# Fused attention, expert and gated layers: when the kept halves come back, where the second batch's k and the probabilities are made, and one place for a tile's transposes

## The chip, the cores and the metric

One core of a Trainium2 chip runs the whole program. The metric is the device time of one execution in microseconds, lower is better. Runs of this kernel lie within 0.5 us of each other.

## The reference

Three layers follow one another. The inputs are float32, and 2304 tokens (4 batches of 576) pass through all three.

```python
# attention: q, k, v are (4, 8, 576, 64); k and v are averaged over groups of 8 positions (576 -> 72)
k_p = k.reshape(B, H, 72, 8, D).mean(axis=3);  v_p = v.reshape(B, H, 72, 8, D).mean(axis=3)
scores = q @ k_p.T / sqrt(64);  attn = softmax(scores);  x = attn @ v_p      # -> (2304, 512)
# four experts, each token weighted by its probabilities
p = domain_probs / (domain_probs.sum(-1, keepdims=True) + 1e-9)              # (2304, 4)
for e in range(4):
    out += p[:, e:e+1] * (relu(x @ w1[e]) @ w2[e])                           # 512 -> 1024 -> 512
# gated layer
h = ((x @ w1) * (x @ w2)) @ w3;  result = h @ w_out                          # 512 -> 1024 -> 512
```

## The kernel before, in words

Every product is formed from a high and a low part of each operand (`mm3`, lines 111 to 114: three matmuls for one), so that a matrix has two tiles, `...h` and `...l`. The high part is a copy on ScalarE (ACT), the low part a subtraction on VectorE (DVE) or GpSimd (POOL): `hi_lo`, lines 116 to 118, whose line 118 thus shows up for many tiles.

**Lead and hooks.** Tokens go in blocks of 384, three tiles of 128. `lead` is a list of pieces that makes the first block's attention before any expert work: pooled k (`pool_k`: DVE sums groups of 8, POOL multiplies with a mask into `kb`), its transposes (`make_kT`, TensorE), transposed q (`make_qT`), scores, exponentials, normalisation, the transposes of the probabilities (`attn_T`, reached by `do_turn`), and `attend`, which gives the block's operand `xh`, `xl`. Tile 3 is the first of the next block, and tile 4 the first that needs the second batch's pooled k (`k1`, `kT1`). Its q needs a load that interleaves rows (`load_qb`) and one transpose on DVE (line 388).

The expert work goes in units: (expert, block, one of 8 column chunks `fc`). A unit makes 12 matmuls of the first product (`expert_h`, lines 568 to 573, result `hhh`, `hhl`) and, two units later, 12 of the second. Between these halves of units lie the numbered `hooks`: `between(n)` runs what was put into hook n, so that the remaining attention work fills in among the expert matmuls. All work on one engine runs in the order in which the program is written. Loads are issued from SyncE's queue (SP) in the order of the list `loads`, which follows the order of lead and hooks. In the hooks and in all the gated layer's set-up only two PSUM banks (`spare[:2]`) are left for scores, kT and transposes of probabilities.

**The w stage** (units of kind "w", around 887 to 935 us) multiplies w3 with w_out while the operands of the gated layer's first product are prepared: `weights_of(j, 0)` and `weights_of(j, 1)` split four blocks of weights into parts; the second of these calls splits a tile `s` of 128 x 1024 into `wh`, `wl`, four times in this stage. In every unit DVE also makes `w3hl`, which the unit's second matmul (line 113) reads.

**The gated layer** takes the 4 batches twice, for two halves of the inner dimension. In the first half a batch's tiles (4 or 5 of 128 x 512) are written to `half_d` in memory; in the second half each is loaded again (`earlier`), added on DVE to the tile's PSUM result and stored to `out` (`give`). The tiles' matmuls are run for three of four chunks for all tiles, then tile by tile for the fourth, each followed by its `give`. `rawpool` has four buffers.

The functions that the change touches:

Of the kernel before, what the change touches and what calls it, by code (L numbers as in the profile page):

```python
# [17 lines left out]
def fused_kernel(  # L18
# [246 lines left out]
    with tc.manual_schedule():  # L265
# [57 lines left out]
            nc.sync.dma_start(r[:NK, :], v[b, h].rearrange("(j r) d -> j (r d)", r=POOL))  # L323
            in_t["v", b, h] = r

        def pool_k(b, c):
            if c == 0:
                kb_t[b] = ap.tile([P, NCH, 2, D], F32, tag="kb", name="kb", bufs=1)
            r, n = in_t.pop(("k", b, c))
            kp = ap.tile([P, D], F32, tag="kp", name="kp")  # L330
            if n < P:
                nc.gpsimd.memset(kb_t[b][n:, c], 0.0)
            nc.vector.tensor_reduce(kp[:n], r[:n, :].rearrange("p (r d) -> p d r", d=D), axis=AX.X, op=ALU.add)  # L333
            nc.gpsimd.tensor_tensor(kb_t[b][:n, c], kp[:n].unsqueeze(1).broadcast_to([n, 2, D]),
                                    mk[:n, c].unsqueeze(2).broadcast_to([n, 2, D]), op=ALU.mult)

        def make_kT(b, g0, g1):
            if g0 == 0:
                kT_t[b] = ap.tile([P, NCH * P], F32, tag="kT", name="kT")
            pt = bank("kT_ps")  # L340
            for c in range(g0, g1):
                nc.tensor.transpose(pt[:, (c - g0) * P:(c - g0 + 1) * P],
                                    kb_t[b][:, c].rearrange("p a d -> p (a d)"), ident)
            nc.scalar.activation(kT_t[b][:, g0 * P:g1 * P], pt[:, :(g1 - g0) * P], AF.Copy)
# [117 lines left out]
            if what:  # L462
                done(what)

        def do_k(b):
            return [(("k", b, c), lambda c=c: pool_k(b, c)) for c in range(NCH)]

        def do_kT(b):
            return [(None, lambda: make_kT(b, 0, 4)), (None, lambda: make_kT(b, 4, NCH))]

        def do_v(b, *engs):
            return [(("v", b, h), lambda h=h: pool_v(b, h, engs[h % len(engs)])) for h in range(H)]
# [33 lines left out]
        def weight(eng):  # L506
            return [(None, lambda: stream.split(eng))]
# [4 lines left out]
        def warm(n):  # L512

            def f():
                pw = bank("warm")
                for _ in range(n):
                    nc.tensor.transpose(pw[:, :P], ident, ident)
            return [(None, f)]

        k0, kT0, k1, kT1 = do_k(0), do_kT(0), do_k(1), do_kT(1)  # L520
        v0 = do_v(0, GP, GP, VE, GP, GP, GP, GP, GP)
        lead = (warm(W0) + k0[:4] + kT0[:1] + k0[4:] + do_qT(0) + kT0[1:] + do_qT(1) + do_scores(0) + do_exps(0) + v0[:2]
                + do_qT(2) + do_scores(1) + v0[2:3] + do_exps(1) + do_scores(2) + v0[3:5] + do_normalise(0) + do_exps(2)
                + v0[5:6] + do_normalise(1) + warm(W1) + do_turn(0) + do_normalise(2, VE) + v0[6:]
                + warm(W2) + do_turn(1) + weight(GP) + do_turn(2) + do_attend(0) + weight(VE) + k1[:2] + do_qT(3))

        hooks = [[] for _ in range(2 * FC * ATT_BLOCKS + 4)]
        hooks[1] = k1[2:] + do_qT(TPB + 1)
        hooks[2] = kT1[:1]
        hooks[3] = kT1[1:] + [(None, probs)]  # L530
        hooks[5] = [(None, probs_T)]
        for t in range(TPB, NTILE + 1):
            h = hooks[3 * (t - TPB) + (t > TPB):]
            if t < NTILE:
                h[0] += do_scores(t) + do_exps(t)
                if t > TPB:
                    h[1] += do_qT(t + 1)
                one, two = do_normalise(t)
                h[1].append(one)
                h[2].append(two)  # L540
            if t > TPB:
                one, two = do_turn(t - 1)
                h[1].insert(0, one)
                h[2].insert(0, two)
                if t % TPB == 0:
                    h[3] += do_attend(t // TPB - 1)
        for b, at_v, at_k in ((1, 3, None), (2, 15, 11), (3, 26, 23)):
            for n, piece in enumerate(do_v(b, GP)):
                hooks[at_v + n].append(piece)
            if at_k:  # L550
                for n, piece in enumerate(do_k(b)):
                    hooks[at_k + n // 2].append(piece)
                hooks[at_k + 4] += do_kT(b)
        first = [("k", 0, c) for c in range(NCH)] + [("q", t) for t in range(LEAD)] + [("v", 0, h) for h in range(H)]
        loads += first + [what for what, _ in lead + sum(hooks, []) if what and what not in first]

# [82 lines left out]
        def weights_of(j, n=None):  # L639

            def split(src, at, m, eng):
                src = src.rearrange("p a b c -> p (a b c)") if len(src.shape) == 4 else src.rearrange("p a c -> p (a c)")
                hi_lo(*(t[:, at:at + m].rearrange("p a b c -> p (a b c)") for t in wop_t[j]), src, eng)

            if n != 1:
                left, right = gate_t.pop(j) if j in gate_t else (r for r, _ in stream.take(2))
                wop_t[j] = tuple(late["wops"].tile([P, 7, 2, P], F32R, tag=t, name=t) for t in ("wh", "wl"))
                s = parts[j] = late["small"].tile([P, 4, 2, P], F32, tag="t", name="s", bufs=2)
                sub, add = ALU.subtract, ALU.add
                nc.vector.tensor_tensor(s[:, 0], right[:, :2], right[:, 2:], op=add)  # L650
                nc.vector.tensor_tensor(s[:, 1], s[:, 0], left[:, :2], op=sub)
                nc.vector.tensor_tensor(s[:, 2], left[:, :2], right[:, :2], op=sub)
                nc.vector.tensor_tensor(s[:, 3], left[:, 2:], s[:, 1], op=sub)
                split(left, A11, 2, nc.vector)
                split(right[:, 2:], A22, 1, nc.vector)
                stream.fill()
            if n != 0:
                split(parts.pop(j), S1, 4, nc.gpsimd)

        xr_t, xo_t, xo_next, sums_t, stores = {}, {}, {}, {}, []  # L660
        B0, T0 = slice(B11, B22 + 1), slice(T1, T4 + 1)
# [140 lines left out]
        def made(u):  # L802

            kind, key, fc = u
            if kind == "e":
                e, i = key
                if e == 0 and i == 0:
                    if fc + LAG < FC:
                        stream.split(nc.vector)
                    stream.split()  # L810
                if i == NB - 1:
                    stream.split()
                if e == 0 and i == ATT_BLOCKS and fc == 3:
                    enter_late()
                if dec and fc in (4, 5, 6, 7):
                    rounding.step(SCRATCH + 4 * FC)
                if e == E - 1:
                    if i == NB - 1 and fc == 0:
                        rounding.flush()
                        assert rounding.finished()  # L820
                        stream.fill()
                    if i > 0 and fc == 4:
                        store_acc(i - 1)
                    if i == NB - 1 and fc == FC - 1:
                        enter_wide()
# [127 lines left out]
        for half in range(2):  # L953
            for b in range(B):
# [34 lines left out]
                if b % 2:  # L989
                    tiles = tiles[1:] + tiles[:1]  # L990
                banks = [bank_r("g2") for _ in tiles]
                halves = {}

                def run(m, js):
                    t, get = tiles[m]
                    for j in js:
                        wh, wl = w34_t[half * NJ + j]
                        g = get(j)
                        mm3(banks[m], g[:, 0], g[:, 1], wh[:, 0], wl[:, 0], j == 0, j == NJ - 1)

                def give(m):
                    t, _ = tiles[m]
# [12 lines left out]
                        nc.sync.dma_start(half_d[t], ob)  # L1015

                def earlier(m):
                    if half and m < len(tiles):
                        halves[m] = rawpool.tile([P, DM], F32, tag="raw", name="half")
                        nc.sync.dma_start(halves[m], half_d[tiles[m][0]])  # L1020

                earlier(0)
                earlier(1)
                if half == 0 and b < B - 2:
                    for kc in range(2):
                        load_x(acc_d, b + 2, kc)
                for m in range(len(tiles)):
                    run(m, range(NJ - 1))
                for m in range(len(tiles)):
                    run(m, [NJ - 1])  # L1030
                    give(m)
                    if swap and m in (1, 3):
                        weights_of(2 + m // 2)
                    earlier(m + 2)
                    if m == 1:
                        put_away()
                if not last:
# [37 lines left out]
```

## Time and profile before

| what | value |
|---|---|
| median of 3 runs | 1226.5 us (1226.33 to 1226.85) |
| the profiled execution | 1226.71 us, of which its span is 1225.0 us |
| TensorE matmul busy (PE) | 1198.9 us, 98% of the span |
| TensorE weight load busy (PEld) | 1152.3 us, 94% |
| DVE / POOL / ACT busy | 667.6 / 369.3 / 277.6 us |
| mean granted clock of TensorE | 0.996 of full speed |

TensorE is the busy engine. What another engine does costs time only where TensorE waits for it, where the first matmuls have to wait for their operands, or behind the last matmul. So the places to read are the few in which PE is not busy, and what it waits for there.

### The profile page before, as it was taken

To read this page: it belongs to the slowest core of one execution; us is meant where nothing else is said; L and a number is where in the kernel's file an instruction comes from. 1 tells how busy PE (TensorE), PEld (TensorE's weight loads), DVE (VectorE), ACT (ScalarE), POOL (GpSimd) and SP (SyncE) were. 2 spreads that over 40 slices of the span, in tenths; PEclk is the share of its full clock that TensorE was granted. 3 is DMA by queue.
4 is the path that set the end of the run, shared out by engine and by line. 5 is a ranking of instruction groups with operands and counts; after the bars stand their busy time and mean duration, and the time that the engine had idled before them with its cause. 6 is when DMAs were issued, how large, how long until landed. Compare 5 with 4: busy or idle time off the path is not lost.

```text
span 1225.0 us, 18777 instructions
## 1 busy us (share of the span) xinstructions
PE 1198.9 (98%) x7089; PEld 1152.3 (94%) x7089; DVE 667.6 (54%) x1489; ACT 277.6 (23%) x535; POOL 369.3 (30%) x432
## 2 busy tenths in 40 slices
PE   7899999999999999999999999999998999999996
PEld 6799989999999999999999999999987999999995
DVE  6887544444444556454444444444287767775453
ACT  4443331131111113111112211111253333231110
POOL 5764300043222236222225522211422222341121
PEclk9999999999999999999999999999999999999999
DMA  8853102143112245222114322123365443944642
GB/s 202 230 143 95 52 5 69 56 131 101 52 42 59 59 101 153 59 57 49 49 52 128 108 84 81 56 84 102 110 217 177 155 169 122 338 166 170 217 155 68
DMA packets 147758, 138.47 MB, mean 113 GB/s; under 512 B 48524, under 2 KB 114644, under 8 KB 147668
## 3 DMA queue, kind: packets, MB, share of 16 engines
q1 hardware_dynamic: 147668, 137.28, 36.8%
q8 instruction: 55, 0.90, 0.3%
q14 instruction: 35, 0.29, 0.1%
HBM read 96.05 MB, written 41.19 MB: 112 GB/s over the span
## 4 chain that ended last, share of the span: by engine, by line
PE 90%; DVE 4%; DMA 2%; POOL 1%; issue 1%; ACT 1%; SPq 1%; DVEq 0%; POOLq 0%; ACTq 0%
PE g L113 24%; PE g L114 24%; PE g L112 24%; PE s L112 5%; PE s L114 5%; PE s L113 5%; PE x_ps L447 1%; PE at_ps L435 1%; PE sc L401 1%; DVE w3hl L118 1%; DMA raw<-w 1%; DMA half<-half 0%; POOL w2l L118 0%; DMA stacc<-in_v_dram 0%; DVE kp L333 0%
## 5 line engine op out<-in xcount | busy, mean ns | idle before, releaser
L572 DVE SCALAR_TENSOR_TENSOR hhl<-g,hhh 128x384 fp32r<-128x384 f32 x192 | 106.7, 556 | 365.1 <-ACT hhh L571 365.0
L112 PE MATMUL g<-xl,w1h 128*128 128x384 f32 x768 | 261.5, 340 | 0.5 <-DVE xl L118 0.5
L113 PE MATMUL g<-xh,w1l 128*128 128x384 f32 x768 | 260.0, 339 | 0.0
L112 PE MATMUL g<-hhl,w2h 128*128 128x384 f32 x768 | 259.7, 338 | 0.2 <-DVE part L592 0.2
L114 PE MATMUL g<-xh,w1h 128*128 128x384 f32 x768 | 259.7, 338 | 0.0
L113 PE MATMUL g<-hhh,w2l 128*128 128x384 f32 x768 | 258.0, 336 | 0.0
L114 PE MATMUL g<-hhh,w2h 128*128 128x384 f32 x768 | 257.9, 336 | 0.0
L571 ACT ACTIVATE hhh<-g 128x384 fp32r<-128x384 f32 x192 | 94.5, 492 | 579.6 <-PE g L114 553.7
L224 POOL TENSOR_TENSOR dtmp<-dtmp 128x256 f32<-128x256 f32 x80 | 58.8, 735 | 407.5 <-DVE dtmp L223 366.3
L112 PEld LDWEIGHTS g<-xl,w1h 128*128 128x128 f32 x768 | 144.6, 188 | 2.0 <-DVE xl L118 1.8
L112 PEld LDWEIGHTS g<-hhl,w2h 128*128 128x128 f32 x768 | 144.2, 188 | 0.9 <-DVE part L592 0.7
L113 PEld LDWEIGHTS g<-xh,w1l 128*128 128x128 f32 x768 | 144.7, 188 | 0.0
L114 PEld LDWEIGHTS g<-xh,w1h 128*128 128x128 f32 x768 | 144.5, 188 | 0.0
L113 PEld LDWEIGHTS g<-hhh,w2l 128*128 128x128 f32 x768 | 144.4, 188 | 0.0
L114 PEld LDWEIGHTS g<-hhh,w2h 128*128 128x128 f32 x768 | 144.1, 188 | 0.0
L118 POOL TENSOR_TENSOR g<-c,g 128x576 fp32r<-128x576 f32 x32 | 47.4, 1481 | 193.9 <-ACT g L117 193.9
L593 POOL TENSOR_TENSOR acc<-acc,part 128x384 f32<-128x384 f32 x72 | 71.2, 1021 | 72.0 <-DVE part L592 72.0
L112 PE MATMUL s<-xol,wh 128*128 128x288 f32 x308 | 91.1, 296 | 0.0
L114 PE MATMUL s<-xoh,wh 128*128 128x288 f32 x308 | 91.0, 296 | 0.0
L113 PE MATMUL s<-xoh,wl 128*128 128x288 f32 x308 | 90.6, 294 | 0.0
L117 ACT ACTIVATE g<-c 128x576 fp32r<-128x576 f32 x32 | 21.9, 686 | 160.5 <-DVE c L947 160.5
L112 PEld LDWEIGHTS s<-xol,wh 128*128 128x128 f32 x308 | 57.9, 188 | 0.4
(146 smaller groups left out, 1790.7 us busy)
## 6 DMA issues: line engine op xcount, KB each, us to landing
raw<-in_moe_w_dram SPq DMA_DIRECT2D x64, 256.0 KB
din<-in_moe_w_dram SPq DMA_DIRECT2D x64, 256.0 KB
p<-p SPq DMA_DIRECT2D x24, 192.0 KB
acc<-acc SPq DMA_DIRECT2D x6, 768.0 KB
xr<-acc SPq DMA_DIRECT2D x16, 288.0 KB
half<-ob SPq DMA_DIRECT2D x18, 256.0 KB
half<-half SPq DMA_DIRECT2D x18, 256.0 KB
out_dram<-half SPq DMA_DIRECT2D x18, 256.0 KB
```

Source lines behind the costliest of these rows:

```text
L112: nc.tensor.matmul(ps, lh, rl, start=first, stop=False)
L113: nc.tensor.matmul(ps, ll, rh, start=False, stop=False)
L114: nc.tensor.matmul(ps, lh, rh, start=False, stop=last)
L117: nc.scalar.activation(hi, src, AF.Copy)
L118: (lo_eng or nc.vector).tensor_tensor(lo, src, hi.bitcast(F32), op=ALU.subtract)
L224: nc.gpsimd.tensor_tensor(a, a, b, op=ALU.add)
L401: nc.tensor.matmul(sc[off:off + n, (hp % 2) * W:(hp % 2 + 1) * W], qT[:, hp, off:off + n], kT_t[b][:, hp * W:(hp + 1) * W], start=True, st ...
L435: nc.tensor.transpose(pt[:NK, g * P:(g + 1) * P], e[:, half * G + g, :], ident)
L447: nc.tensor.matmul(px[a * D:(a + 1) * D, off:off + n], vp_t[b][:NK, 2 * hp + a], at_t[i, hp // 2][:NK, 2 * (hp % 2) + a, off:off + n], sta ...
L571: nc.scalar.activation(hh, ps, AF.Relu)
L572: nc.vector.scalar_tensor_tensor(hl, ps, 0.0, hh.bitcast(F32), op0=ALU.max, op1=ALU.subtract)
L593: nc.gpsimd.tensor_tensor(acc_t[i][:, c], acc_t[i][:, c], part, op=ALU.add)
```

## The change

Six things change. (1) In the lead, the four DVE operations on the probabilities and their transpose (`probs`, `probs_T`) and tile 3's q transpose go ahead of block 0's `attend`; the first three chunks of `k1` go there too and are summed on POOL, by three additions each, in place of one DVE reduction. (2) kT1 is made in pieces of 3 and 2 chunks at hooks 3 and 4 (before: 4 and 1 at hooks 2 and 3), and tile 4's q transpose moves from hook 1 to 3. (3) In the hooks a table `at` sets the place of each tile; the two halves of a tile's transposes stand in one hook, two after the next tile's scores, and the transposes of kT for batches 2 and 3 have hooks without transposes of probabilities. `enter_late` comes one unit later, as attention ends five hooks later. (4) In the w stage the low part of the 128 x 1024 split goes from POOL to DVE. (5) In the second half of the gated layer all of a batch's kept halves are loaded at the batch's begin, four into `rawpool` and the fifth into a buffer of `small`. (6) The last tile of all is made in two pieces of 256 columns, each with its own PSUM bank, addition and store.

```diff
-        def pool_k(b, c):
+        def pool_k(b, c, eng=nc.vector):
...
-            nc.vector.tensor_reduce(kp[:n], r[:n, :].rearrange("p (r d) -> p d r", d=D), axis=AX.X, op=ALU.add)
+            if eng is nc.vector:
+                eng.tensor_reduce(kp[:n], r[:n, :].rearrange("p (r d) -> p d r", d=D), axis=AX.X, op=ALU.add)
+            else:
+                eng.tensor_tensor(r[:n, :256], r[:n, :256], r[:n, 256:], op=ALU.add)
+                eng.tensor_tensor(r[:n, :128], r[:n, :128], r[:n, 128:256], op=ALU.add)
+                eng.tensor_tensor(kp[:n], r[:n, :64], r[:n, 64:128], op=ALU.add)
...
-        k0, kT0, k1, kT1 = do_k(0), do_kT(0), do_k(1), do_kT(1)
+        k0, kT0, k1, kT1 = do_k(0), do_kT(0), do_k(1, 3), do_kT(1, 3)
...
-                + warm(W2) + do_turn(1) + weight(GP) + do_turn(2) + do_attend(0) + weight(VE) + k1[:2] + do_qT(3))
+                + warm(W2) + do_turn(1) + weight(GP) + do_turn(2) + [(None, probs), (None, probs_T)] + do_qT(3) + k1[:3] + do_attend(0)
+                + weight(VE))
...
-        hooks[1] = k1[2:] + do_qT(TPB + 1)
-        hooks[2] = kT1[:1]
-        hooks[3] = kT1[1:] + [(None, probs)]
-        hooks[5] = [(None, probs_T)]
...
+        hooks[1] = k1[3:]
+        hooks[3] = kT1[:1] + do_qT(TPB + 1)
+        hooks[4] = kT1[1:]
+        at = {TPB: 0, TPB + 1: 5, TPB + 2: 8}
+        for i in range(2, NB):
+            for n, gap in enumerate((-3, 0, 3)):
+                at[i * TPB + n] = 10 * i - 6 + gap
...
+        for t in range(TPB, NTILE):
+            hooks[at[t + 1] + 2] += do_turn(t)
...
-                split(parts.pop(j), S1, 4, nc.gpsimd)
+                split(parts.pop(j), S1, 4, nc.vector if n else nc.gpsimd)
...
-                if e == 0 and i == ATT_BLOCKS and fc == 3:
+                if e == 0 and i == ATT_BLOCKS and fc == 4:
...
+                pieces = [slice(0, DM // 2), slice(DM // 2, DM)]
+                over = bank_r("g2") if last else None
...
+                def give_part(m, cols):
...
+                    nc.vector.tensor_tensor(ob[:, cols], bank[:, cols], ob[:, cols], op=ALU.add)
+                    nc.sync.dma_start(out[t * P:(t + 1) * P, cols], ob[:, cols])
...
-                earlier(0)
-                earlier(1)
+                if half:
+                    for m in range(len(tiles)):
+                        earlier(m)
...
+                    for cols in pieces if last and m == len(tiles) - 1 else [slice(0, DM)]:
+                        run(m, range(NJ - 1), cols)
...
+                    if last and m == len(tiles) - 1:
+                        for cols in pieces:
+                            run(m, [NJ - 1], cols)
+                            give_part(m, cols)
+                        break
...
-                    earlier(m + 2)
```

The first place is DVE at the end of the lead, from block 0's `xl` on; `kp` is a pooled chunk of k1, `hhl` the low part of an expert unit's result. Before:

```order
L118 TENSOR_TENSOR xl<-x_ps,xh 128x384 x4
L118 TENSOR_TENSOR w1l<-raw,w1h 128x512
L333 TENSOR_REDUCE kp<-stxl 128x64 x2
L388 STREAM_TRANSPOSE qT<-stxh 128x4x4x32
L572 SCALAR_TENSOR_TENSOR hhl<-g_429,hhh 128x384
L118 TENSOR_TENSOR w1l<-raw,w1h 128x512
L413 TENSOR_REDUCE mx<-sc 128x4
```

And in the changed kernel, from the operation that follows tile 2's normalisation on:

```order
L499 TENSOR_REDUCE sp<-dp 128x18
L500 TENSOR_SCALAR sp<-sp 128x18
L501 RECIPROCAL sp<-sp 128x18
L502 TENSOR_TENSOR dp<-dp,sp 128x72
L393 STREAM_TRANSPOSE qT<-stxh 128x4x4x32
L118 TENSOR_TENSOR xl<-x_ps,xh 128x384 x4
L118 TENSOR_TENSOR w1l<-raw,w1h 128x512
L576 SCALAR_TENSOR_TENSOR hhl<-g_453,hhh 128x384
L118 TENSOR_TENSOR w1l<-raw,w1h 128x512
L418 TENSOR_REDUCE mx<-sc 128x4
```

The probabilities and tile 3's qT moved ahead of `xl`, and the two `kp` are gone from between `w1l` and qT (and one more from behind).

The second place is DVE in the w stage, around the second 128 x 1024 split. Before:

```order
L653 TENSOR_TENSOR s<-gate,s 128x256
L118 TENSOR_TENSOR wl<-gate,wh 128x512
L118 TENSOR_TENSOR wl<-gate,wh 128x256
L118 TENSOR_TENSOR w3hl<-raw,w3hh 128x384 x2
L681 TENSOR_TENSOR t<-xr 128x288
```

In the changed kernel:

```order
L657 TENSOR_TENSOR s<-gate,s 128x256
L118 TENSOR_TENSOR wl<-gate,wh 128x512
L118 TENSOR_TENSOR wl<-gate,wh 128x256
L118 TENSOR_TENSOR w3hl<-raw,w3hh 128x384
L118 TENSOR_TENSOR wl<-s,wh 128x1024
L118 TENSOR_TENSOR w3hl<-raw,w3hh 128x384
L685 TENSOR_TENSOR t<-xr 128x288
```

The 128 x 1024 `wl`, which stood on POOL, now stands between two `w3hl`.

The third place is SP's queue in the last batch: loads of kept halves (`half<-half`) and stores to the output. Before:

```order
L1020 DMA half<-half_9337 128x512
L1020 DMA half<-half_9338 128x512
L1012 DMA out_dram<-half 128x512
L1020 DMA half<-half_9339 128x512
L1012 DMA out_dram<-half 128x512
L1020 DMA half<-half_9340 128x512
L1012 DMA out_dram<-half 128x512
L1020 DMA half<-half_9336 128x512
L1012 DMA out_dram<-half 128x512 x2
```

In the changed kernel:

```order
L1036 DMA half<-half_9343 128x512
L1036 DMA half<-half_9344 128x512
L1036 DMA half<-half_9345 128x512
L1036 DMA half<-half_9346 128x512
L1036 DMA half<-half_9342 128x512
L1026 DMA out_dram<-half 128x512 x4
L1013 DMA out_dram<-half 128x256 x2
```

All five loads now stand ahead of the batch's first store, and the last tile has two stores of half the width.

## Rows read from the trace of the kernel before

**Rows 1.** The page: TensorE's granted clock in 40 slices, in tenths.

```profile
PEclk9999999999999999999999999999999999999999
```

**Rows 2.** Waits of PE, whole kernel: total us, times, longest.

```profile
PE g L113 <- DVE w3hl L118: 2.5, 3, 1.1
...
PE g L112 <- DVE w34l L118: 0.8, 1, 0.8
...
PE kT_ps L342 <- ACT at L438: 0.7, 2, 0.4
PE g L112 <- DVE xl L118: 0.5, 1, 0.5
```

**Rows 3.** Timeline of PE, 33 to 53 us: start, us, what, [idle before].

```profile
33.39 1.25 PE L401 MATMUL sc<-kT,qT 128*128 128x144 f32 x8 [2.49 <-DVE qT L388]
...
39.69 0.33 PE L342 MATMUL kT_ps<-ident,kb 128*128 128x128 f32 x1 [0.59 <-POOL kb L334]
...
46.68 0.60 PE L435 MATMUL at_ps<-ident,e 128*72 128x128 f32 x4 [1.17 <-DVE e L414]
...
52.25 1.14 PE L401 MATMUL sc<-kT,qT 128*128 128x144 f32 x8
```

**Rows 4.** Windows: stretch, length, PE, PEld, DVE, ACT, POOL busy, granted clock, DMA.

```profile
34.38:38.12 3.74, 3.74 (x15) 3.71 (x14) 3.67 (x7) 0.89 (x2) 0.40 (x1) 0.54 1.00 259
39.78:42.03 2.25, 2.25 (x13) 2.00 (x13) 2.18 (x6) 0.72 (x3) 1.64 (x2) 1.00 0.89 178
```

**Rows 5.** Timeline of DVE, 23 to 45 us.

```profile
23.27 1.00 DVE L426 TENSOR_TENSOR e<-e,sm 128x576 f32<-128x576 f32 x1
...
27.26 2.52 DVE L118 TENSOR_TENSOR xl<-x_ps,xh 128x384 fp32r<-128x384 f32 x4 [3.00 <-ACT xh L117]
...
30.36 1.98 DVE L333 TENSOR_REDUCE kp<-stxl 128x64 f32<-128x512 f32 x2
32.25 1.09 DVE L388 STREAM_TRANSPOSE qT<-stxh 128x512 f32<-128x512 f32 x1
...
41.88 1.50 DVE L118 TENSOR_TENSOR w1l<-raw,w1h 128x512 fp32r<-128x512 f32 x1
...
44.35 0.26 DVE L497 TENSOR_TENSOR dp<-dp,sp 128x72 f32<-128x72 f32 x1
```

**Rows 6.** Timeline of POOL, 14 to 43 us.

```profile
14.21 0.72 POOL L354 TENSOR_TENSOR stacc<-stacc 72x256 f32<-72x256 f32 x1
...
15.82 0.72 POOL L354 TENSOR_TENSOR stacc<-stacc 72x256 f32<-72x256 f32 x1
...
26.54 1.28 POOL L118 TENSOR_TENSOR w1l<-raw,w1h 128x512 fp32r<-128x512 f32 x1
...
31.53 0.40 POOL L334 TENSOR_TENSOR kb<-kp,mk 128x128 f32<-128x128 f32 x1 [3.72 <-DVE kp L333]
```

**Rows 7.** Timeline of the w stage, DVE and POOL, 906 to 914 us.

```profile
906.62 1.36 DVE L118 TENSOR_TENSOR xol<-t,xoh 128x1152 fp32r<-128x1152 f32 x1
...
910.77 0.56 DVE L118 TENSOR_TENSOR w3hl<-raw,w3hh 128x384 fp32r<-128x384 f32 x1
...
911.09 2.50 POOL L118 TENSOR_TENSOR wl<-s,wh 128x1024 fp32r<-128x1024 f32 x1 [10.63 <-ACT wh L117]
...
911.52 2.48 DVE L118 TENSOR_TENSOR w3hl<-raw,w3hh 128x384 fp32r<-128x384 f32 x1 [0.20 <-ACT w3hh L117]
```

**Rows 8.** Timeline of the end, 1212 to 1225 us.

```profile
1212.95 1.39 DVE L1011 TENSOR_TENSOR half<-g,half 128x512 f32<-128x512 f32 x2 [9.79 <-PE g L114]
...
1215.30 0.40 PE L114 MATMUL g<-w34h,edge 128*128 128x512 f32 x1
...
1218.28 0.42 SPq L1020 DMA_DIRECT2D half<-half  x1
...
1219.13 3.22 SPq L1012 DMA_DIRECT2D out_dram<-half  x2
1221.30 0.69 DVE L1011 TENSOR_TENSOR half<-g,half 128x512 f32<-128x512 f32 x1 [2.19 <-DMA half<-half]
```

More of the change, by code (lines that the diff above doesn't have):

```diff
@@ L463, in do, with do_k, do_kT @@
                 done(what)
[L465 to L469, printed above, removed]
+        def do_k(b, on_pool=0):
+            return [(("k", b, c), lambda c=c: pool_k(b, c, nc.gpsimd if c < on_pool else nc.vector)) for c in range(NCH)]
+        def do_kT(b, cut=4):
+            return [(None, lambda: make_kT(b, 0, cut)), (None, lambda: make_kT(b, cut, NCH))]
         def do_v(b, *engs):
@@ L524, in fused_kernel @@
                 + v0[5:6] + do_normalise(1) + warm(W1) + do_turn(0) + do_normalise(2, VE) + v0[6:]
-                + warm(W2) + do_turn(1) + weight(GP) + do_turn(2) + do_attend(0) + weight(VE) + k1[:2] + do_qT(3))
-        hooks = [[] for _ in range(2 * FC * ATT_BLOCKS + 4)]
-        hooks[1] = k1[2:] + do_qT(TPB + 1)
-        hooks[2] = kT1[:1]
-        hooks[3] = kT1[1:] + [(None, probs)]
-        hooks[5] = [(None, probs_T)]
[L532 to L547, printed above, removed]
+                + warm(W2) + do_turn(1) + weight(GP) + do_turn(2) + [(None, probs), (None, probs_T)] + do_qT(3) + k1[:3] + do_attend(0)
+                + weight(VE))
+        hooks = [[] for _ in range(2 * FC * ATT_BLOCKS + 7)]
+        hooks[1] = k1[3:]
[5 more added lines that the diff above has]
+                at[i * TPB + n] = 10 * i - 6 + gap
+        at[NTILE] = at[NTILE - 1] + 4
+        for t in range(TPB, NTILE):
+            one, two = do_normalise(t)
+            for after, pieces in ((0, do_scores(t) + do_exps(t)), (1, do_qT(t + 1) if t > TPB else []),
+                                  (2 if t == TPB else 1, [one]), (3 if t == TPB else 2, [two])):
+                hooks[at[t] + after] += pieces
+        for t in range(TPB, NTILE):
+            hooks[at[t + 1] + 2] += do_turn(t)
+        for i in range(1, NB):
+            hooks[10 * i + 4][:0] = do_attend(i)
+        for b, at_v, at_k, at_kT in ((1, 3, None, None), (2, 15, 15, 20), (3, 26, 25, 30)):
             for n, piece in enumerate(do_v(b, GP)):
@@ L552, in fused_kernel @@
                     hooks[at_k + n // 2].append(piece)
-                hooks[at_k + 4] += do_kT(b)
+                hooks[at_kT] += do_kT(b)
         first = [("k", 0, c) for c in range(NCH)] + [("q", t) for t in range(LEAD)] + [("v", 0, h) for h in range(H)]
@@ L991, in fused_kernel, with run @@
                 banks = [bank_r("g2") for _ in tiles]
+                pieces = [slice(0, DM // 2), slice(DM // 2, DM)]
+                over = bank_r("g2") if last else None
                 halves = {}
-                def run(m, js):
+                def run(m, js, cols=slice(0, DM)):
                     t, get = tiles[m]
@@ L998, in run @@
                         g = get(j)
-                        mm3(banks[m], g[:, 0], g[:, 1], wh[:, 0], wl[:, 0], j == 0, j == NJ - 1)
+                        bank = banks[m] if cols.start == 0 else over
+                        mm3(bank[:, cols], g[:, 0], g[:, 1], wh[:, 0, cols], wl[:, 0, cols], j == 0, j == NJ - 1)
+                def give_part(m, cols):
+                    t, _ = tiles[m]
+                    ob = halves[m]
+                    bank = banks[m] if cols.start == 0 else over
+                    nc.vector.tensor_tensor(ob[:, cols], bank[:, cols], ob[:, cols], op=ALU.add)
+                    nc.sync.dma_start(out[t * P:(t + 1) * P, cols], ob[:, cols])
                 def give(m):
@@ L1017, in earlier @@
                 def earlier(m):
-                    if half and m < len(tiles):
+                    if m < 4:
                         halves[m] = rawpool.tile([P, DM], F32, tag="raw", name="half")
-                        nc.sync.dma_start(halves[m], half_d[tiles[m][0]])
-                earlier(0)
-                earlier(1)
+                    else:
+                        halves[m] = late["small"].tile([P, DM], F32, tag="xr", name="half", bufs=2)
+                    nc.sync.dma_start(halves[m], half_d[tiles[m][0]])
+                if half:
+                    for m in range(len(tiles)):
+                        earlier(m)
                 if half == 0 and b < B - 2:
@@ L1027, in fused_kernel @@
                 for m in range(len(tiles)):
-                    run(m, range(NJ - 1))
+                    for cols in pieces if last and m == len(tiles) - 1 else [slice(0, DM)]:
+                        run(m, range(NJ - 1), cols)
                 for m in range(len(tiles)):
+                    if last and m == len(tiles) - 1:
[3 more added lines that the diff above has]
+                        break
                     run(m, [NJ - 1])
```

## Prediction

> **What bounds the kernel now.** I read the page first: TensorE's matmuls are busy for 98% of the span, and its granted clock stands at 9 in each of 40 slices [rows 1]. A change that adds no matmul work can then only win back the few microseconds in which PE waits, and what lies behind its last matmul. The list of PE's waits says which they are [rows 2], and the timelines of PE, DVE, POOL and SP around them say why. There are three places.
>
> In the lead and the first units, 31 to 47 us, PE waits 2.49 us for tile 3's q transpose on DVE, 0.59 us for a masked k chunk and 1.17 us for tile 4's exponentials [rows 3]. Behind the first wait the granted clock is 0.54, that is mostly the lower of its two levels (1.2 of 2.4 GHz), over a stretch of one first product (twelve matmuls) and a few transposes, which takes 3.74 us; a like stretch at clock 1.00 takes 2.25 us [rows 4]. That is 1.5 us more.
>
> In the w stage, PE waits three times, 2.5 us in all, for `w3hl`, and once 0.8 us for a bank that `w34l` frees [rows 2].
>
> At the end, the last matmul ends at 1215.70 (1215.30 and 0.40), and the span only at 1225.0. Between them a chain runs through SP: the load of the last kept half is issued at 1218.28, the last addition waits 2.19 us for it and runs at 1221.30, and its store ends the program [rows 8]. That is 9.3 us without a matmul.
>
> **The change part by part.** The sums are made against the profiled execution, 1226.71 us, which is 0.2 us above the median.
>
> *Lead and first units.* What goes: 2.49, 1.5, 0.59 and 1.17 us, together 5.75 us. The probabilities take 1.2 us of DVE (from the end of the operation at 41.88 to 44.61) and qT 1.09 us [rows 5]; in their new place DVE is idle from 24.27 to 27.26 us, so 2.3 us go into a gap of 3.0 us, if dp and tile 3's q have arrived. q's load is issued ahead of two k loads of 256 KB that stood before it, so it is not later than it was. PE's first product of unit 0 ends as before at 30.9 us (33.39 less 2.49), and the scores follow at once at the full clock.
>
> What comes: three k chunks on POOL. Three additions take 1.61 us (one chain begins at 14.21, the next at 15.82) and the mask 0.40 us; those rows have 72 partitions, and I take the same for 128. POOL is free at 27.82 us (26.54 and 1.28), so the third chunk is ready at 27.82 + 3 x 2.01 = 33.85 us [rows 6]. PE comes to its transpose at 30.9 + 1.0 for the scores + 2.25 for a first product = 34.15 us: just in time. Then chunks 3 and 4 and tile 4's q: before, DVE went from the scores' start at 33.39 to 41.88 [rows 3, 5] through softmax, three sums of k, qT, sums and `hhl`. Now one sum of k (1.0) is gone and a `w1l` comes in; its row reads 1.50 us, and I take 0.7 to 1.5. The softmax also starts up to 1.2 us later after the scores, since one more `w1l` and `hhl` stand ahead. So qT of tile 4 is done 8.2 to 10.2 us after 30.9, at 39.1 to 41.1 us; PE needs it at 34.15 + 2.25 + 0.5 + 2.25 = 39.2 us. New waits: 0 to 2 us; I take 1.2 us, past the middle because POOL's additions run beside DVE the whole time. Net -4.6 us. The bounds: -5.75 with no new wait; -1.75 if the new wait is as long as the old one and brings the low clock with it (4.0 us back).
>
> *One place for a tile's transposes.* No matmul is added or removed. The waits of kT's transposes on ACT's copies (0.7 us) come where kT stood in the hook of a tile's second transposes, and now it has one of its own. `attend` now always stands ahead of a second product rather than of the next first product, whose bank it shares; that takes the 0.5 us [rows 2]. I take -1.0 us; bounds 0 and -1.2. The later `enter_late` moves no work off another engine that PE waits for: 0.
>
> *The w stage.* POOL's 128 x 1024 subtraction runs 2.50 us from 911.09. The `w3hl` that starts on DVE beside it takes 2.48 us and ends when POOL does, the one before it 0.56 us [rows 7]. So each of the four splits on POOL holds a `w3hl` up by 1.9 us. On DVE the split costs itself: 1.36 us for 1152 columns gives 1.2 us for 1024 [rows 7]. DVE thus comes out 0.7 us ahead per split, and PE's waits, four of 0.8 us on average at the end of the stage, lie behind three or four splits, so most of the 3.3 us goes: -2.8 us. The bounds: -3.3 us; and if `w3hl` were slow for another cause, DVE, already the engine that PE waits for, would have 1.2 us more before each of the last two waits: +2.4 us.
>
> The Trainium skill (SBUF — State Buffer, section "SBUF: two separate sides") states that DVE, in an operation with two SBUF inputs, and a GpSimd operation take one shared port pair in turn, and that the loser waits for the whole instruction. The row of 2.48 us beside 2.50 agrees with it. The same rule speaks against the lead's part, where sums of k move to POOL beside DVE's `w1l`; what the row of 41.88 (1.50 us) would make of that is the first rival.
>
> *The end.* The kept halves are there from the batch's begin: nothing else is loaded in the last batch, and the first addition comes after 9.79 us of idle DVE [rows 8]. So DVE goes on from 1212.95 with four additions at 0.70 us (two take 1.39), to 1215.73, and two of half the width, of 0.35 to 0.69 us each; at 0.4 us DVE ends at 1216.5. Before, from DVE's end at 1221.99 to the span's end there are 3.0 us; for a store of half the size I take 2.9 us. End at 1219.4: -5.6 us. The bounds: the last tile's 24 matmuls of 256 columns at half the time of a wide one cost nothing more; at 0.14 us each, as those of 144 columns at 52.25 [rows 3], they take 3.4 us against 2.8 (12 at 0.23): 0.6 us later. With additions of 0.69 us that makes -4.4 us; with a store that takes half as long, -7.0 us. In the other batches of that half PE shows no wait [rows 2], so that earlier loads give nothing there; they stand behind the next batch's operands in SP's queue and delay none of them: 0.
>
> The sum: -4.6 - 1.0 - 2.8 - 5.6 = -14.0 us; 1226.7 - 14.0 = 1212.7, and 1212.5 us against the median.
>
> **Rivals.** *The lead's gain is given back.* POOL's nine additions of k and DVE's `w1l` hold each other up, the third chunk or tile 4's q comes 2.5 us late and the low clock returns. For it: POOL is in time by only 0.3 us, and `w1l` at 41.88 took 1.50 us. Against it: waits of 0.59 and 1.17 us brought no low clock (window 39.78 to 42.03 at 1.00). The lead then gives -1.75 us: 1215.4 us.
>
> *DVE bounds the w stage.* The +2.4 us above in place of -2.8: 1217.7 us. Against it: the long `w3hl` ends with POOL's operation.
>
> *Slower than before.* A tile's eight transposes now fill both banks at once, and what next needs a bank waits for two copies. Such a wait took 0.35 us (0.7 in two); if it also brought the low clock, 1.5 us more. Fifteen tiles are turned this way: 15 x 1.85 = 27.8 us, which gives 1240 us; from eight such tiles on the 14.0 us are gone. Against it: half a unit (2.25 us) stands between a tile's transposes and the next use of the banks, and the two waits of before left the clock at 9 in their slices.
>
> *More than forecast.* No new wait in the lead, and all waits of the w stage and hooks gone: -5.75 - 1.2 - 3.3 - 6.2 = -16.5 us, 1210 us.
>
> *The change doesn't do what it says* can only be so in the hooks: both places were hidden, 1213.5 us, inside the forecast's own range.
>
> **How the numbers follow.** The forecast, 1212.5 us (own range 1210.7 to 1214.5): 0.60. Lead given back, 1215.4: 0.16. DVE bounds the w stage, 1217.7: 0.09. More than forecast, 1210: 0.12. Slower: 0.03. The range 1208.5 to 1217 leaves out the w stage rival, the slow one and little else. A difference of under 0.2% (2.5 us) can't be told from none here. Faster 0.96, the same 0.01, slower 0.03.
>
> **What would show each step.** In the changed profile: scores of tile 3 right behind unit 0's first product at about 31 us, with the granted clock at 1.00 from there on, and tile 4's scores waiting under 2 us; second product of unit 1 done near 46 us. No wait of kT on ACT. `w3hl` at 0.56 us throughout the w stage, `wl` of 128 x 1024 at 1.2 us on DVE, and PE's waits there under 0.6 us together. At the end, six additions without a wait on DMA, and 3.7 us between the last matmul and the span's end. The forecast is wrong if PE's waits for DVE in the first units sum to over 3 us, if a split on DVE makes a `w3hl` late that was not, or if additions in the last batch still wait for loads.

## The result, and the profile after

The changed kernel takes 1215.01 us (median of 4 runs, 1212.77 to 1215.82; before, beside it, 1226.41): ratio 0.9904, 95% interval 0.9887 to 0.9921. In a later set it took 1216.69 us (5 runs, 1213.13 to 1218.15; before 1226.88), ratio 0.9916 [0.9902, 0.9931]. The forecast was 1212.5 us, range 1208.5 to 1217. Executions of the changed kernel spread over 3.1 and 5.0 us in the two sets, those of before beside them over 0.9 and 2.3; the profiled one is the shortest, 1212.77 us with a span of 1211.1 us, so its profile alone would make the forecast look exact; that closeness is luck of the execution. The 52 executions of the kernel before that were run beside these kernels lie between 1225.14 and 1228.95 us, so the 0.5 us in which its first three lay was too narrow a measure of its scatter.

TensorE's waits in this profile, to be held against [rows 2]:

```profile
PE sc L406 <- ACT kT L349: 2.4, 2, 1.4
PE g L112 <- ACT w3hh L117: 1.0, 1, 1.0
PE g L113 <- DVE w3hl L118: 0.6, 1, 0.6
```

The waits for tile 3's qT and of kT on ACT's copies are gone, those for `w3hl` fell from 2.5 to 0.6 us. Two are new: tile 4's scores wait for ACT's copies of kT, and the w stage once for `w3hh`. The timeline of PE in the first units, which answers to [rows 3]:

```profile
29.60 1.14 PE L406 MATMUL sc<-kT,qT 128*128 128x144 f32 x8
...
33.59 0.33 PE L347 MATMUL kT_ps<-ident,kb 128*128 128x128 f32 x1 [0.54 <-POOL kb L339]
...
40.43 0.71 PE L406 MATMUL sc<-kT,qT 128*64 128x144 f32 x8 [1.43 <-ACT kT L349]
42.12 0.71 PE L406 MATMUL sc<-kT,qT 128*64 128x144 f32 x8 [0.98 <-ACT kT L349]
47.03 1.04 PE L440 MATMUL at_ps<-ident,e 128*72 128x128 f32 x8
```

Tile 3's scores (29.60) follow unit 0's first product without a wait, as forecast. ACT's timeline shows why tile 4's (40.43) wait:

```profile
39.37 0.63 ACT L117 ACTIVATE w2h<-raw 128x512 fp32r<-128x512 f32 x1 [4.18 <-DMA raw<-in_moe_w_dram]
39.90 0.47 ACT L349 ACTIVATE kT<-kT_ps 128x384 f32<-128x384 f32 x1
```

ACT stands 4.18 us before a `w2h` whose load has not landed; the copy of kT, whose transposes were done at 33.9, stands behind it in ACT's order. And SP's queue shows why the load is late:

```profile
29.57 0.74 SPq L137 DMA_DIRECT2D raw<-in_moe_w_dram  x1
30.40 0.41 SPq L509 DMA_DIRECT2D p<-pT  x1
30.91 1.75 SPq L378 DMA_DIRECT2D stxh<-in_q_dram  x4
32.75 0.86 SPq L323 DMA_DIRECT2D stxl<-in_v_dram  x2
34.59 0.30 SPq L323 DMA_DIRECT2D stxh<-in_v_dram  x1
34.98 0.35 SPq L135 DMA_DIRECT2D raw<-in_moe_w_dram  x1
```

Line 137 loads a w1 block, line 135 a w2 block. Between them stand the store of the probabilities, tile 5's q and three v loads of the second batch, for staging spots that POOL's early sums of k free. In the profile before, that w2 load was issued at 32.33:

```profile
32.33 0.45 SPq L135 DMA_DIRECT2D raw<-in_moe_w_dram  x1
```

In the w stage DVE now makes the 128 x 1024 split itself, in 1.22 us, and the `w3hl` behind it takes 0.55 us, where [rows 7] had 2.48:

```profile
905.01 1.22 DVE L118 TENSOR_TENSOR wl<-s,wh 128x1024 fp32r<-128x1024 f32 x1
906.15 0.55 DVE L118 TENSOR_TENSOR w3hl<-raw,w3hh 128x384 fp32r<-128x384 f32 x1
```

The end, which answers to [rows 8]; the additions now run without a wait on a load:

```profile
1204.43 2.79 DVE L1025 TENSOR_TENSOR half<-g,half 128x512 f32<-128x512 f32 x4 [9.86 <-PE g L114]
1206.91 0.28 PE L114 MATMUL g<-w34h,edge 128*128 128x256 f32 x1
1207.14 0.75 DVE L1012 TENSOR_TENSOR half<-g,half 128x256 f32<-128x256 f32 x2
1207.69 0.88 SPq L1013 DMA_DIRECT2D out_dram<-half  x2
```

The last matmul ends at 1207.19 (1206.91 and 0.28), the span at 1211.1: 3.9 us, where it was 9.3.

### The profile page after: what moved, and what is told of

It reads as the page before. It is cut to its first block, busy times and chain, and to the rows that moved or that the text cites. A ratio compares the mean times of both kernels' runs of the same rounds, so it can differ in the third digit from the quotient of the medians.

```text
span 1211.1 us, 18810 instructions
## 1 busy us (share of the span) xinstructions
PE 1196.3 (99%) x7101; PEld 1152.9 (95%) x7101; DVE 665.4 (55%) x1491; ACT 276.3 (23%) x535; POOL 365.3 (30%) x437
## 4 chain that ended last, share of the span: by engine, by line
PE 92%; DVE 3%; DMA 2%; issue 1%; POOL 1%; ACT 1%; DVEq 0%; SPq 0%; POOLq 0%; ACTq 0%
PE g L113 25%; PE g L112 25%; PE g L114 25%; PE s L112 5%; PE s L114 5%; PE s L113 5%; PE x_ps L452 1%; PE sc L406 1%; PE at_ps L440 1%; DMA raw<-w 1%; DVE kp L334 0%; DMA raw<-in_moe_w_dram 0%; DMA gate<-gate 0%; POOL w2l L118 0%; DMA gate<-dtmp 0%
## 5 line engine op out<-in xcount | busy, mean ns | idle before, releaser
L113 PEld LDWEIGHTS s<-xoh,wl 128*128 128x128 f32 x308 | 57.9, 188 | 0.2
```

The source lines that it names most:

```text
L113: nc.tensor.matmul(ps, ll, rh, start=False, stop=False)
```

## Experiments

**The parts one by one.** `e1_tail`, `e2_w_dve` and `e3_lead_hooks` are the kernel before with some hunks of the change only: the two of the gated layer's tail; the line below; and the hunks of `pool_k`, lead, hooks and `enter_late`.

```diff
-                split(parts.pop(j), S1, 4, nc.gpsimd)
+                split(parts.pop(j), S1, 4, nc.vector if n else nc.gpsimd)
```

> The kernel before, with the tail edits alone (kept halves loaded at a batch's begin, last tile in two pieces). Theory, the end's term: the last additions no longer wait for their loads and the last tile ends with half an addition and half a store; last matmul to span end 3.7 to 4.0 us where before it was longer, everything ahead of about 1196 us unmoved; 5.4 to 5.6 us less than before, about 1221. Rival: part of what the changed kernel's end gained came from loads that the earlier stages had shifted; then 3 us less at most, 1223 or more.

Measured: 1221.13 us (1220.89 to 1221.82), before 1226.61, 5.5 us less, 0.9958 [0.9946, 0.997]. From the last matmul's end (1215.31) to the span's (1219.2) it is 3.9 us. The end's term stands, alone and whole.

> The kernel before, with the low parts of 128x1024 in the stage of the last weights taken from GpSimd to VectorE and nothing else. Theory, a two-input subtraction of GpSimd holds VectorE's for its length: the 1.9 to 2.5 us low parts of w3 go to 0.56, TensorE's waits in this stage fall by 2 to 2.8 us, time 1223.6 to 1224.4. Rival, VectorE is only lengthened by 1.2 us for each of them: no gain, 1226.4 to 1228.8.

Measured: 1223.67 us (1223.01 to 1226.35), 2.9 us less, 0.9982 [0.9974, 0.9991]; from the first 128 x 1024 split on every `w3hl` of 384 columns takes 0.55 us, and TensorE's waits in this stage are 0.7 and 0.5 us. POOL's operation was the cause; the rival falls.

> The kernel before, with the rebuilt lead and the moved transposes, without the edits of the last weights and of the tail. Theory: first units 3.3 to 4.4 us less (1.1 of the 4.4 seen was only an earlier first reduction on VectorE, on an unchanged list of instructions), transposes 1.0 to 1.7 less: together 4.3 to 6.1, 1220.3 to 1222.1. Rival, the first units' gain is given back by the wait for tile 4's scores: 2.4 us or less of gain, 1224 or more.

Measured: 1224.10 us (1221.08 to 1226.76), 2.5 us less, 0.9978 [0.997, 0.9987]. Less than expected, with a spread of 5.7 us. In its profile the scores of tile 4 wait 3.42 and 0.98 us for ACT's kT, and the granted clock from 46 to 50 us is 0.50.

**The old lead with everything else.** `e6_hooks_only` is the changed kernel with the lead and the first hooks of before:

```diff
-        k0, kT0, k1, kT1 = do_k(0), do_kT(0), do_k(1, 3), do_kT(1, 3)
+        k0, kT0, k1, kT1 = do_k(0), do_kT(0), do_k(1), do_kT(1)
...
-                + warm(W2) + do_turn(1) + weight(GP) + do_turn(2) + [(None, probs), (None, probs_T)] + do_qT(3) + k1[:3] + do_attend(0)
-                + weight(VE))
+                + warm(W2) + do_turn(1) + weight(GP) + do_turn(2) + do_attend(0) + weight(VE) + k1[:2] + do_qT(3))
...
-        hooks[1] = k1[3:]
-        hooks[3] = kT1[:1] + do_qT(TPB + 1)
-        hooks[4] = kT1[1:]
+        hooks[1] = k1[2:] + do_qT(TPB + 1)
+        hooks[2] = kT1[:1]
+        hooks[3] = kT1[1:] + [(None, probs)]
+        hooks[5] = [(None, probs_T)]
```

> The changed kernel with the first block's k, q and probabilities prepared where they were before; the places of the tiles' transposes from tile 4 on, the edits of the last weights and of the end as changed. Theory, by the runs of the single edits (5.5 for the end, 2.9 for the last weights, 1.0 to 1.7 for the transposes) 1216.3 to 1217.2 and a spread as before's, under 2 us. Rival, the new lead carries nothing in the median: 1214.5 to 1215.5.

Measured: 1216.77 us (1215.85 to 1217.09), before 1226.88: 10.1 us less, spread 1.2 us. With 5.5 and 2.9 for the tail and the w stage, the transposes' places give 1.7 us. The changed kernel, run beside it, took 1216.69: there the new lead carries 0.1 us. Against the first set (11.4 us less) it carries 1.3, in `e3_lead_hooks` 0.8. All nine executions of the changed kernel (1212.77 to 1218.15, median 1215.82) against these four put its gain at 0.95 us, with a 95% interval from 3.3 us gained to 1.1 lost: neither nothing nor the forecast's bound of 1.75 is ruled out.

**The changed kernel again**, `e7_after_again`, no edit.

> The changed kernel itself, more runs and another profiled execution. Theory, its spread comes from the first units: an execution near 1215 shows the first expert weight that is loaded after the lead issued 2 us later than 29.57, tile 4's scores waiting 3.5 us or more and a stretch of 4 to 5 us at the lower clock behind them; an execution near 1213 shows none of these. Rival, the spread lies elsewhere in the program and the first 60 us are alike.

Its profile is of an execution of 1216.69 us: SP's first expert load after the lead, the `w2h` ahead of the copy of kT on ACT, tile 4's scores on PE, and the windows from 42 us on (stretch, length, busy times, granted clock, DMA share, GB/s).

```profile
31.80 0.40 SPq L137 DMA_DIRECT2D raw<-in_moe_w_dram  x1
```

```profile
41.21 0.63 ACT L117 ACTIVATE w2h<-raw 128x512 fp32r<-128x512 f32 x1 [3.85 <-DMA raw<-in_moe_w_dram]
```

```profile
42.27 0.71 PE L406 MATMUL sc<-kT,qT 128*64 128x144 f32 x8 [2.95 <-ACT kT L349]
43.96 1.23 PE L406 MATMUL sc<-kT,qT 128*64 128x144 f32 x8 [0.98 <-ACT kT L349]
```

```profile
42.00:46.00 4.00, 2.75 (x19) 2.09 (x20) 2.76 (x6) 2.35 (x6) 3.92 (x4) 0.74 0.50 151
46.00:50.00 4.00, 4.00 (x21) 4.00 (x20) 1.07 (x3) 1.85 (x4) 3.77 (x7) 0.83 0.57 173
```

The load is issued 2.23 us later than 29.57, the wait is 3.93 us in place of 2.41, and behind it the granted clock is 0.74 and 0.83, TensorE's lower level for part of these 8 us. By my estimate, against the full clock throughout, that loses up to (0.26 + 0.17) x 4 = 1.7 us, over some 3.4 us at half speed (expected: 4 to 5). In the 1212.77 us execution both windows read 1.00. At tile 8's transposes this execution is 3.4 us behind the first (96.71 and 93.31), of the 3.9 us by which it ends later. The theory holds: the difference is made in the first 97 us.

**What holds tile 4's scores.** `e4_late_release` gives the spots of three k chunks back a hook later, so that the w2 load stands ahead of three v loads; `e8_k_on_dve` sums those chunks on DVE (`do_k(1, 0)`).

```diff
-            if what:
+            if what and what not in kept_back:
...
+        hooks[0] = [(None, give_back)]
```

> The changed kernel, but the staging spots of batch 1's first three k chunks are given back one hook later, so that on SyncE's queue the load of the second w2 block stands ahead of three v loads, not behind them; no engine's list is altered but SyncE's. Theory, the new 2.4 us wait of tile 4's scores comes from that load (issued 34.98, its w2h on ScalarE at 39.37, the copies of kT behind it): load issued near 32.8, landed near 37.2, copies of kT by 38.5, scores of tile 4 without a wait; 1.5 to 2.4 us below the changed kernel, 1212.6 to 1213.5. Rival, VectorE's qT of tile 4 (the prediction's cause) or GpSimd's sums hold the scores: the wait stays over 1.5 us and the time stays at 1214.5 to 1215.5.

Measured: 1215.13 us (1213.03 to 1217.44), no gain that the scatter lets show. The profile is of the slowest of the four executions. The w2 load is issued right behind tile 5's q now (35.66), but in this execution all of SP's queue is 3.2 us later (w1 at 32.82), and another operation ends the first wait:

```profile
PE sc L406 <- DVE qT L393: 2.0, 1, 2.0
PE sc L406 <- ACT kT L349: 1.6, 1, 1.6
```

DVE's qT, the prediction's cause, is late itself for a load: it stands behind a `w1l` whose `w1h` on ACT waited 2.84 us for DMA. My theory of one blocked load was too narrow: in this profile every early load of expert weights is late.

> The changed kernel, but batch 1's first three k chunks are summed on VectorE as the other two are. Theory, weight loads late on SyncE's queue: VectorE has 3 us more work ahead of tile 3's maxima and of the third chunk, but GpSimd's low part of w2 comes earlier; within 1 us of the changed kernel, 1214 to 1216. Rival, GpSimd's 9 additions are what holds the first units: 1.5 us or more below the changed kernel.

Measured: 1214.59 us (1213.12 to 1216.07). That is 0.4 us below the changed kernel's first set but 2.1 us below the set run beside it (1216.69), and the rival asked for 1.5: with spreads of 3 to 5 us the time leaves it open. The trace speaks against it. DVE's sums move a wait of 1.2 us to unit 0's `xl`, and tile 4's scores, with waits of 0.65 and 1.26 us, still wait for ACT's kT, which stands behind a `w2h` that waits 3.14 us for its load.

**Is it SP's queue, or the transfers?** `e5_dp_rows` loads the probabilities in long runs and drops their transposes; `e9_weights_first` holds back v and q loads until unit 0 is made; `e10_both` does both.

```diff
-        nc.sync.dma_start(dp, domain_probs.rearrange("(t p) e -> p t e", p=P))
+        nc.sync.dma_start(dp, domain_probs.rearrange("(t p) e -> t p e", p=P))
```

```diff
+        newest = {"q": LEAD, "qb": TPB + 1, "k": 1, "v": 0}
...
-                if spots[kind_of(what)]:
+                if what[1] <= newest.get(what[0], NTILE) and spots[kind_of(what)]:
...
+        hooks[0] = [(None, newest.clear)]
```

> The changed kernel, but the domain probabilities are loaded and kept with one tile of tokens to a partition (18 runs of 2 KB where there were 2304 of 16 bytes) and normalised in that layout, so that their transpose on TensorE and its copy on ScalarE go; the same values are stored. Theory, SyncE's queue: the issue that follows the short runs took 5.6 to 5.9 us of the queue where the other three of that group of four take 0.45 each; without it the loads of the expert weights leave 4 us or more earlier, tile 4's scores wait under 1 us in every execution, the clock stays at its higher level, 1210 to 1212, spread under 1.5 us. Rival, the loads are late for the time they take to land, not for the queue: waits of 2.4 us or more and 1214 to 1216 as the changed kernel.

Measured: 1215.18 us (1214.16 to 1216.03). The group of four q issues behind the probabilities fell from 5.7 to 5.9 us to 2.5, but the eight issues of tile 4's q behind them took 6.56 us in place of 5.18 to 6.02. The one issue right behind the probabilities, which takes 4.50 us in the changed kernel's first profile where the other three of its group take some 0.43, is what shortened (0.31 to 0.34 here). The time did not go to the weights: w1 is issued at 29.85, w2 at 35.37, and tile 4's scores wait 1.27 and 0.98 us. So the theory falls by its own sign. The rival, that landing and not the queue sets the pace, is left but not shown, as the queue as a whole was not made shorter.

> The changed kernel, but until block 0's first unit is done no load of batch 1's v or of a q tile after tile 4 is issued: SyncE's queue brings the next three blocks of expert weights ahead of three v loads, tile 5's q and three more v loads. Theory, those loads ahead of the second w2 block make its first part on ScalarE late, and with it the copies of kT: w1 issued by 30.8, w2 by 32, tile 4's scores waiting 1 us or less for the first group, no stretch at the lower clock: 1212.5 to 1214 against 1215 to 1216.7 for the changed kernel. Rival, the DMA engines are full to 38 us whatever the order (0.81 to 1.03 busy), so that the load lands as late: 1214.5 to 1216.5. Another rival, the v loads that are put off hold batch 1's sums and tile 6: 1216 or more.

Measured: 1215.02 us (1214.31 to 1215.88). The first wait went as the theory said, and came back later. PE in its profile:

```profile
41.50 1.20 PE L406 MATMUL sc<-kT,qT 128*64 128x144 f32 x16 [0.38 <-DVE qT L393]
...
59.69 1.25 PE L406 MATMUL sc<-kT,qT 128*128 128x144 f32 x8 [1.50 <-ACT at L443]
```

ACT, ahead of that `at`, now waits 1.53 us for a w1 load. The loads that were put off come between 38 and 60 us, and the DMA engines are busy for 1.00 of that time (0.79 in the changed kernel's first profile). The order of loads moved the wait; it did not remove it.

> The run before it with the domain probabilities in 18 runs of 2 KB as well, which gave 2 us of SyncE's queue in one profile and no time in the median by itself. Theory, both together bring the weights in time in every execution: 1211.5 to 1213, spread under 1.5 us. Rival, what bounds is the landing: 1214.5 to 1216.

Measured: 1215.70 us (1215.26 to 1216.85), as `e9_weights_first`: waits of 0.4 and 1.3 us at the same two places. The time is the rival's. In the trace tile 4's `w2h` (35.77) no longer waits for its load; the wait is back at 59.62, for a w1 load whose `w1h` waits 1.67 us.

**The w stage's rest, and the clock.** `e11_stores_later` moves four stores; `e12_warm` adds transposes ahead of tile 4's scores.

```diff
-        for n in (14, 18):
-            early[n].append(put_away)
+        for n in (14, 22):
+            early.setdefault(n, []).append(put_away)
```

```diff
+        def keep_warm(n):
+            pw = g1_bank("warm")
+            for _ in range(n):
+                nc.tensor.transpose(pw[:, :P], ident, ident)
...
+        hooks[5] = [(None, lambda: keep_warm(12))]
```

> The changed kernel, but the second four stores of the kept operands, in the stage of the last weights, are issued four units later, behind the last w3 load on SyncE's queue. Theory, the wait that is left in that stage (0.97 and 0.58 us in one profile, 1.6 to 2.0 together in the others) is for a w3 load that stands behind those stores: the load of the last block issued near 915.4, where it was 918.13, TensorE's waits from 915 to 930 us under 0.7, 1 us less: 1213.8 to 1215. Rival, VectorE bounds this stage by then (three low parts of 1.22): the waits stay over 1.4 us and the time at 1215 to 1216.7.

Measured: 1215.95 us (1214.88 to 1216.99). TensorE waits once in that stage, 0.6 us, where 1.2 to 1.7 us had stayed in the others with this edit: the stores cost 0.6 to 1.1 us of wait. The median doesn't show it, since the first units vary by more; its profile has tile 4's scores waiting 2.92 and 0.98 us and the clock at 0.73 and 0.84 from 42 to 50.

> The run before it, and 12 transposes of the identity (some 1.3 us) on TensorE ahead of tile 4's scores, into a bank that is free by then. Theory, the lower clock in the slower executions of the first units (0.74 to 0.83 from 42 to 50 us) comes of TensorE's standing still 3.5 to 4 us behind unit 2, and costs some 2 us by the matmuls' 0.32 for 0.173: with work in the gap the clock stays up, spread under 2 us, median 0.5 to 1.5 us below the run before it. Rival, the clock falls for another reason and the transposes lie on the path: 0.3 to 1.3 us above it.

Measured: 1212.71 us (1211.37 to 1214.54), before 1226.37, ratio 0.9889 [0.9873, 0.9906]; 3.2 us below the run before it, with a spread of 3.2 us. The expectation missed twice: it had 0.5 to 1.5 us below, and a spread under 2. PE, and the same two windows:

```profile
39.77 0.34 PE L114 MATMUL g<-hhh,w2h 128*128 128x384 f32 x1
39.94 1.47 PE L345 MATMUL warm<-ident 128*128 128x128 f32 x12
41.73 0.71 PE L411 MATMUL sc<-kT,qT 128*64 128x144 f32 x8 [0.32 <-ACT kT L354]
43.43 0.71 PE L411 MATMUL sc<-kT,qT 128*64 128x144 f32 x8 [0.98 <-ACT kT L354]
```

```profile
42.00:46.00 4.00, 3.02 (x27) 2.55 (x24) 2.95 (x6) 2.26 (x6) 3.84 (x6) 1.00 0.53 151
46.00:50.00 4.00, 4.00 (x28) 3.94 (x27) 2.96 (x4) 2.56 (x5) 3.77 (x6) 1.00 0.54 158
```

The weights are as late as in the run before it (`w2h` at 40.67, there 40.91); the transposes fill the gap, tile 4's scores come no later (41.73, there 41.97), and the clock stays at its higher level. But this profile does not show that the transposes kept it there. Unit 2's second product ends at 40.1 here (39.05 in the run before it), so without the transposes the waits would have been some 1.6 and 0.98 us, close to the 1.43 and 0.98 us of the changed kernel's first profile, whose clock stayed up with no transposes in the gap; in the run before it they were 2.92 and 0.98. Nor does the time of its four executions follow their mean granted clock (0.997 at 1212.02 us, 0.999 at 1214.54). Its median is the lowest of all kernels here; the changed kernel was not run beside it (1215.01 and 1216.69 in other sets).

One row stands in every profile with the new places of transposes: tile 8's transposes. It dates what the first 95 us cost (us from the span's start):

| kernel | tile 3's scores | tile 8's transposes | between |
|---|---|---|---|
| changed, 1212.77 us | 29.60 | 93.31 | 63.7 |
| `e5_dp_rows` | 29.82 | 93.56 | 63.7 |
| `e8_k_on_dve` | 31.99 | 94.41 | 62.4 |
| `e12_warm` | 30.70 | 94.63 | 63.9 |
| `e9_weights_first` | 31.71 | 94.95 | 63.2 |
| `e10_both` | 30.60 | 94.96 | 64.4 |
| old lead (`e6_hooks_only`) | 32.81 | 95.69 | other order |
| `e11_stores_later` | 30.30 | 96.41 | 66.1 |
| changed, 1216.69 us | 30.58 | 96.71 | 66.1 |
| `e4_late_release` | 30.91 | 97.99 | 67.1 |
| `e3_lead_hooks` | 31.26 | 98.91 | 67.7 |

The four below the old lead are the four whose clock fell; the six above it are those whose clock stayed up from 38 to 60 us. Against this one profile of the old lead the new one gains up to 2.4 us or loses up to 3.2, by execution; the old lead's clock falls too (0.82 and 0.76 from 30 to 38 us), and the profile is of the fastest of its four executions (1215.85).

## Why the prediction was right, and where not

- **The end** (-5.6): -5.5, by the steps named; 3.9 us behind the last matmul for 3.7.
- **The w stage** (-2.8): -2.9. Mechanism and size hold: no `w3hl` stands beside a split on POOL, and the split costs DVE 1.2 us. "Under 0.6 us together" of rest was too low: 1.2 to 1.7 us stayed, 0.6 to 1.1 us of it for a w3 load behind stores in SP's queue (`e11_stores_later`).
- **One place for transposes** (-1.0, bounds 0 and -1.2): -1.7, by difference of medians, so with their scatter. From 60 to 900 us the first profile of the changed kernel shows no wait of PE at all; before it had 0.7, 0.5 and two of 0.2, together 1.6, which agrees. (The digits of [rows 1] could not have shown a low clock between: the slice from 30.6 to 61.3 us reads 9 too, with the 3.74 us at 0.54 of [rows 4] in it.)
- **Lead and first units** (-4.6): the step that failed. In the first profile it looks met: the tail's first addition starts 8.5 us earlier (1212.95 in [rows 8], now 1204.43), and less 2.9 and 1.7 for w stage and transposes 3.9 us are the lead's; but 1.1 of these are the first maxima on DVE (12.92 before, 11.80 now), ahead of which nothing changed. By medians the lead gives 0.1 to 1.3 us; the scatter does not rule out the bound of -1.75. The failed step is "What comes", and in its sum the term of new waits, "0 to 2 us; I take 1.2": it measured 3.4 us in the fastest execution (0.54 and 0.47 for POOL's kb, 1.43 and 0.98 for ACT's kT) and more in the one of 1216.69 us. The third chunk on POOL came in time with the forecast (33.53 for 33.85), but PE came to it earlier. I followed tile 4's scores through POOL, DVE and PE, found 0 to 2 us of wait on DVE's qT, and did not follow ACT's copy of kT, which stands behind a `w2h`, nor SP's queue to that block's load. In the profile of 1212.77 us qT was done at 38.54, in time; the copy came at 39.90.
- **The rival "the lead's gain is given back"** (1215.4, 0.16) named the outcome: a wait of some 2.5 us or more with the lower clock. It named the wrong cause; POOL's additions against `w1l` (1.15 us at 28.60) held no product of unit 1 up in the first profile (its matmuls at 30.48 do not wait for that `w1l`). By time, `e8_k_on_dve` leaves POOL's share open.

The terms as measured make -5.5 - 2.9 - 1.7 - (0.1 to 1.3) = -10.2 to -11.4 us, the two medians (the last two terms are differences of medians, so this closes by itself). A sum of runs that doesn't: `e1_tail`, `e2_w_dve` and `e3_lead_hooks` alone make 5.5 + 2.9 + 2.5 = 10.9 us, between the two.

Open: why the early loads land 1 to 3 us apart between executions of the same list; and why `e12_warm` is 3.2 us better than its neighbour in the median, while tile 8's transposes come 1.8 us earlier in the profiles. Loads from a second issuing engine were not tried. Nor was the plainest test of the cause: both copies of kT ahead of the `w2h` in ACT's order. An estimate from the first profile: their transposes are done at 33.9 and 36.9, ACT stands idle from 35.2 to the `w2h` at 39.37, tile 4's qT is done at 38.54 and unit 2's second product at 39.0; and unit 1's second product, up to 2.4 us earlier at some 42.5, would still find POOL's `w2l` done (41.40). So up to 2.4 us of wait could go. As long as this is not run, that ACT's copy holds tile 4's scores is read from the traces and not shown by taking the wait away.

## What to carry to other kernels

When work moves ahead into a start-up phase, follow the loads too: earlier frees let later loads into an in-order queue ahead of ones that are needed sooner, and a copy on ACT is as late as the load of whatever stands ahead of it. Where a phase is bound by transfers, its gain shows in one execution and not in the next; judge it by medians of each part alone, not by one profile. A wait that can't be removed can be filled: the run with cheap transposes in the gap has the lowest median of all, though whether by the clock is not shown.

## What the hardware showed

- Waits of TensorE of 1.43 and 0.98 us (with 0.71 us of work between) left the granted clock at 1.00, as did 1.27 and 0.98 (`e5_dp_rows`) and 0.65 and 1.26 (`e8_k_on_dve`); a single wait of 2.49 us in the kernel before [rows 3, 4], 2.95 and 0.98, or 2.04 and 1.63 us (`e4_late_release`), were followed by half-speed matmuls (0.32 us from one to the next where 0.173 is usual). The Trainium skill (TensorE: Matmul & The Clock Gate, section "HAM oscillation — how this bites in real kernels") says that waits for loads between groups of matmuls let the next group start on the lower clock; the rows with the longer waits agree. That transposes of an identity prevent it is not shown: in the profile of `e12_warm` the gap without them would have been close to one that left the clock up.
- Fewer short runs made one group of issues on SP 3 us shorter and the next one longer (`e5_dp_rows`): I take from it that in the first 38 us an issue's time on the queue goes by the transfers ahead of it (DMA share 0.81 to 0.96 in that profile); no run shows that by itself.
